# Two transposes of k and q on VectorE, each set some instructions later in the queue

## The chip, the cores and the metric

The kernel runs on one core of a Trainium2 chip. The metric is the device time of one execution in microseconds (us), measured in repeated runs. TensorE is PE in the profile, VectorE is DVE, ScalarE is ACT, GpSimd is POOL and SyncE is SP. A DMA is issued by the queue of SP, ACT or POOL.

## The reference

An mLSTM cell over 4 batches of 8 heads, 768 positions and head size 40, and then a feed-forward network (FFN) on its output, 3072 rows of 320 numbers:

```python
for t in range(S):
    m_new = np.maximum(f_gate[:, :, t] + m, i_gate[:, :, t])
    f_stab = np.exp(f_gate[:, :, t] + m - m_new)
    i_stab = np.exp(i_gate[:, :, t] - m_new)
    C = f_stab * C + i_stab * outer(vt, kt)
    n = f_stab * n + i_stab * kt
    y[:, :, t] = sigmoid(o_gate[t]) * (C @ qt) / np.maximum(np.abs(n @ qt), 1.0)
...
h = np.maximum(x @ w_in, 0.0)          # (3072, 320) @ (320, 2048)
return (h * h @ w_out).astype(np.float32)
```

## The kernel before

The recurrence is computed in chunks of 128 positions. There are 24 chunks, six to a batch, numbered from 0 by `s`; the ninth chunk is chunk 8. Within a chunk the sum over positions is a masked product, as in attention. `scores(s)` multiplies k by q on PE into two PSUM banks (L587, L595). `weigh(s)` makes the decay weights W on ACT and POOL in the tile `A_bc` (L510, L479). `weighted(s)` multiplies scores by W on VectorE in two instructions (L609), and the result, P, stands in `A_bc`. `attend_begin(s)` and `attend_end(s)` multiply P by v and the carried state C by the scaled q, and form the new state, on PE (L801, L823, L835). Between these two lies a tiny VectorE instruction on one element (L792), which reads what `attend_begin` wrote last. PE's `attend_end` waits for it. The change's title calls it the marker.

The FFN works on groups of two chunks, `g`. `ffn1_open`, `ffn1_rows` and `ffn1_close` are the first product, done with seven block products instead of eight (L1140, L1173); `ffn2_fast` is the second, in four steps of two products each (L1061). VectorE adds and subtracts the partial results: L1077 for the second product, L1156, L1158 and L1192 to L1195 for the first, and L1056 for the sums of blocks.

From chunk 7 on, k and q come into the layout that the scores need in three steps. `pair_up(s)` copies them into the DRAM scratch `kq_rows`. `load_squares(s)` brings them back as 32x32 squares into the tile `kqT_b[s % 2]` with four DMAs (L399), from SP up to chunk 10, then from ACT for odd chunks and SP for even ones. `turn_kq(s)` turns the squares in place on VectorE:

```python
def turn_kq(s):
    t = kqT_b[s % NKT][:].rearrange("p n j t -> p (n j t)")
    nc.vector.transpose(t, t)
```

It is one instruction over 128 x 1024 numbers (L406) and waits for all four DMAs. `scores(s)` waits for it.

The order is written by hand. Each engine takes its instructions in the order of the program, and waits for the other engines by semaphores. The main loop runs over quarter steps `n`, with `s = 6 + n // 4` and `at = n % 4`. In the steps of an even chunk PE does one group's second product, in those of an odd chunk another group's first one (`fast`). From chunk `EARLY = 10` on the even chunks are `joined`: their scores and their `attend_begin` stand inside the FFN1 of the chunk before. Chunks 8 and 9 are where the loop passes from one order to the other:

- `n = 8` (`s = 8`, `at = 0`): scores of chunk 8, turn of chunk 9, P of chunk 8, then step 0 of the second product of group 1.
- `n = 9`: `attend_begin(8)`, scores of chunk 9, `attend_end(8)`; behind these, in SP's queue, the load of the numerators (`load_num(8)`, L878) and `load_squares(10)`.
- `n = 11`: turn of chunk 10, then step 3 of the second product of group 1, whose last sum is an L1077.
- `n = 12` (`s = 9`, `at = 0`): `ffn1_open(3, 0)`, with L1156 and L1158.
- `n = 13`: `attend_begin(9)` with its marker, `ffn1_rows`, scores of chunk 10, `attend_end(9)`.

Of the kernel before, what the change touches and what calls it, by code (L numbers as in the profile page):

```python
# [29 lines left out]
def kernel(  # L30
# [317 lines left out]
    def load(s):  # L348
        b, c = divmod(s, NB)
        (dk, sk), nat_q, vv = load_parts(s)  # L350
        if s < ROT:
            for dst, src in ((dk, sk), nat_q, vv) if s < KQ_SQ else ((dk, sk), vv):
                nc.sync.dma_start(dst, src[b, :, c * P : (c + 1) * P, :].rearrange("h p d -> p h d"))
            return
        load_k(s)
        load_v(s)
# [47 lines left out]
# [3 lines that stand above are left out]
# [159 lines left out]
    def scores(s, o=(False, False)):  # L566
        d = st[s]

        sc = [bank(o[i]) for i in range(2)]
        d["sc"] = sc  # L570
        if s >= KQ_SQ:
            if s >= ROT:
                d["sc"] = [t.rearrange("p j t -> p (j t)")[:, : 3 * P].rearrange("p (e t) -> p e t", e=2) for t in sc]
            for e in range(2):
                for late_keys in range(2):
                    for c in range(2):
                        for i in range(2):
                            rows = slice(DP * i, DP * i + D)
                            start = e == late_keys == 0
                            if s < ROT:  # L580
                                j, keys = 2 * late_keys + e, HALVES[c]
                                to, t0 = sc[i][HALVES[c], j, :], 0
                            else:
                                j, keys = 2 * (c ^ late_keys) + e, HALVES[late_keys]
                                to = d["sc"][i][HALVES[c], e, slice(0, DP) if late_keys else slice(DP, 3 * DP)]
                                t0 = DP * late_keys
                            nc.tensor.matmul(  # L587
                                to, lhsT=d["kT"][rows, j, keys], rhs=d["qT"][rows, j, t0:], start=start, stop=True,
                                skip_group_check=True,
                            )  # L590
            return
        for j in range(PR):
            for i in range(2):
                rows = slice(DP * i, DP * i + D)
                nc.tensor.matmul(  # L595
                    sc[i][:, j, :], lhsT=d["kT"][rows, j, :], rhs=d["qT"][rows, j, :], start=True, stop=True,
                )
# [285 lines left out]
    def normalise_turned(s):  # L883
        d = st[s]
        N = d["N"].rearrange("p (e half m i r) -> p e half m i r", e=2, half=2, m=2, r=SQ)
        R = D - SQ
        den = N[:, :, 1, :, :, R]
        dm = work.tile([P, H], F32, name="dm")
        dm2 = dm[:].rearrange("p (m e i) -> p e m i", m=2, e=2)
        nc.vector.tensor_scalar(dm2, den, scalar1=-1.0, scalar2=1.0, op0=ALU.mult, op1=ALU.max)  # L890
        nc.vector.tensor_tensor(dm2, dm2, den, op=ALU.max)
        nc.vector.reciprocal(dm[:], dm[:])
        x = d["x"] = work.tile([P, 3 * P], F32, name="x_sb")
        x3 = x[:, :DM].rearrange("p (h d) -> p h d", d=D)
        x4, og = [
            t.rearrange("p (m e i) d -> p e m i d", m=2, e=2) for t in (x3, d["og"])
        ]
        for e in range(2):
            nc.vector.tensor_tensor(x4[:, e, :, :, :SQ], N[:, e, 0], og[:, e, :, :, :SQ], op=ALU.mult)
        for e in range(2):  # L900
            nc.vector.tensor_tensor(x4[:, e, :, :, SQ:], N[:, e, 1, :, :, :R], og[:, e, :, :, SQ:], op=ALU.mult)
        nc.vector.tensor_tensor(x3, x3, dm[:].unsqueeze(2).to_broadcast([P, H, D]), op=ALU.mult)
        nc.vector.tensor_copy(x[:, DM:], x[:, DM - KR : DM])
# [25 lines left out]
    def store_rows(s):  # L929
        t = st[s]["xT"] = xT_half(s).rearrange("p c t -> p (c t)")  # L930
        nc.sync.dma_start(x_d[s].rearrange("c t d -> t c d"), st[s]["x"][:].rearrange("p (c d) -> p c d", c=3))

    def load_rows(s):
        t = st[s]["xT"]
        for r in range(P // SQ):
            nc.sync.dma_start(
                t[r * SQ : (r + 1) * SQ].rearrange("p (b a) -> p b a", a=SQ),
                x_d[s, :, :, r * SQ : (r + 1) * SQ].rearrange("c (n p) a -> p (c n) a", p=SQ),
            )

    def turn_squares(s):
        t = st[s]["xT"]
        nc.vector.transpose(t, t)  # L943
        del st[s]
# [86 lines left out]
    def sums_of_weights(i):  # L1031
        if i < 3:
            T[i] = late.tile([P, NPAIR, DH], F32, name=f"T{i}", bufs=1)[:]
        if i == 0:
            nc.vector.tensor_tensor(T[0], B12, B11, op=ALU.subtract)
        elif i == 1:
            nc.vector.tensor_tensor(T[1], B22, T[0], op=ALU.subtract)
        elif i == 2:
            nc.vector.tensor_tensor(T[2], B21, T[1], op=ALU.subtract)
        else:  # L1040

            nc.vector.tensor_tensor(B12, B22, B12, op=ALU.subtract)
# [118 lines left out]
    def ffn1_rows(g, q, first):  # L1161
        xT, xs = st["xT", g], st["xs"]
        X, Y, V, Z = st["f1"]
        lo, hi = HALVES
        pairs = (
            ((X, lo, xT[lo, 0, 2, :], False), (Y, hi, xT[hi, 1, 2, :], first)),
            ((V, lo, xT[lo, 1, 2, :], first), (Z, hi, xs[hi, 1, :], False)),
        )
        for pair in pairs:
            for n in range(4):  # L1170
                for cols in HALVES:
                    for to, rows, rhs, start in pair:
                        nc.tensor.matmul(  # L1173
                            to[cols, n, :], lhsT=w_in2[rows, 4 * q + n, cols], rhs=rhs,
                            start=(start and n == 0), stop=True, skip_group_check=True,
                        )
# [36 lines left out]
    def do(f, s):  # L1213
        if 0 <= s < NT:
            f(s)
# [97 lines left out]
    for u in range(8):  # L1313
        s = 2 + u // 2
# [119 lines left out]
    EARLY = 10  # L1434
    assert ROUNDED[-1] == len(pieces)

    def joined(s):
        return EARLY <= s < NT and s % 2 == 0

    for n, (which, g, i) in enumerate(parts):  # L1440
        s, at = NB + n // 4, n % 4
# [11 lines left out]
                load_rows(s)  # L1453
        if at == 0 and even and s < EARLY:
            do(scores, s)
            if n > 0:
                do(turn_kq, s + 1)
            do(weighted, s)
        if n == 0:
            turn_kq(7)  # L1460
            pair_up(8)
# [3 lines left out]
        if at == (0 if joined(s) else 1):  # L1465
            if not joined(s):
                do(attend_begin, s)
            if n == 5:
                sums_of_weights(3)
            if even:  # L1470
                do(lambda s: scores(s, ("h" if s < EARLY else False, "h")), s + 1)
            if fast:
                ffn1_rows(g, 0, True)
                if joined(s + 1):
                    scores(s + 1, (False, "h"))
            do(attend_end, s)
            do(decays, s + 1)
            if not even and s > EARLY + 1:
                do(half_tanh, s)
            do(mask, s + 1)  # L1480
            if not even and not fast:
                do(turn_kq, s + 1)
            do(decay_C, s + 1)
            if not fast and not even:
                do(turn_squares, s - 1)
            if s == NB + 2:
                load(s + 3)
            do(store_num, s)
            if s > NB + 1:
                do(load_A, s + 2)  # L1490
            if n == 1:
                normalise_turned(5)
                store_rows(5)
                turn_squares(4)
            if n == 5:
                load_rows(6)
            do(load_num, s)
            if n == 1:
                load_rows(5)
                weigh(7, masked=True)  # L1500
                sums_of_win(2)
            if s + 2 <= EARLY:
                do(load_squares, s + 2)
            if even and s <= NB + 1:
                do(load_A, s + 2)
# [16 lines left out]
        if at == 2 and not fast:  # L1522
            if even and n > 2 and not joined(s):
                do(turn_squares, s - 1)
            do(scale_q, s + 1)
        if at == (1 if joined(s) else 3) and joined(s + 2):
            turn_kq(s + 2)
        if at == 3:
            if s % 4 == 3 and s < EARLY:
# [119 lines left out]
```

## Time and profile before

| | |
|---|---|
| median of 3 runs (lowest, highest) | 489.75 us (489.66, 490.23) |
| the profiled execution's own time | 489.91 us |
| its span, first to last instruction | 488.2 us |
| mean granted clock of PE | 0.992 |
| busy: PE, DVE, ACT, POOL | 476.6, 344.1, 244.0, 224.9 us |
| turns of k and q, L406 | 17 of 1.23 to 1.25 us |

The profile is of one execution. Of its own time of 489.91 us, 1.7 us lie outside the span. An engine's timeline lists its instructions in order of start: start, duration, engine, line, operation, output and inputs, count, and in square brackets how long the engine was idle ahead of it and what ended that. The view of waits adds these idle times up by who waited for whom. The chain of waits follows the end of the span back to what released each step.

### The profile page before, as it was taken

To read this page: it belongs to the slowest core of one execution; us is meant where nothing else is said; L and a number is where in the kernel's file an instruction comes from. 1 tells how busy PE (TensorE), PEld (TensorE's weight loads), DVE (VectorE), ACT (ScalarE), POOL (GpSimd) and SP (SyncE) were. 2 spreads that over 40 slices of the span, in tenths; PEclk is the share of its full clock that TensorE was granted. 3 is DMA by queue.
4 is the path that set the end of the run, shared out by engine and by line. 5 is a ranking of instruction groups with operands and counts; after the bars stand their busy time and mean duration, and the time that the engine had idled before them with its cause. 6 is when DMAs were issued, how large, how long until landed. Compare 5 with 4: busy or idle time off the path is not lost.

```text
span 488.2 us, 15700 instructions
## 1 busy us (share of the span) xinstructions
PE 476.6 (98%) x6389; PEld 444.6 (91%) x6389; DVE 344.1 (70%) x725; ACT 244.0 (50%) x534; POOL 224.9 (46%) x337
## 2 busy tenths in 40 slices
PE   9989999999898999999999999999999999999997
PEld 5877788779798999999999999999999999999997
DVE  7959768888886974775876975965965957635441
ACT  4697897644641651652752751653653651514300
POOL 5454545567881876826746836734833111020000
PEclk9988999999999999999999999999999999999999
DMA  8999998779997698677677686696773322200000
GB/s 174 209 253 265 259 202 209 201 144 230 194 190 108 165 169 164 164 155 155 149 149 153 159 165 145 155 155 128 156 144 87 93 58 82 55 15 15 1 28 27
DMA packets 192839, 69.93 MB, mean 143 GB/s; under 512 B 158144, under 2 KB 181504, under 8 KB 192768
## 3 DMA queue, kind: packets, MB, share of 16 engines
q1 hardware_dynamic: 157424, 56.39, 51.7%
q0 software_dynamic: 6080, 10.16, 9.4%
q10 hardware_dynamic: 29264, 2.39, 4.7%
q8 instruction: 50, 0.82, 0.7%
q14 instruction: 21, 0.17, 0.1%
HBM read 55.69 MB, written 18.92 MB: 153 GB/s over the span
## 4 chain that ended last, share of the span: by engine, by line
PE 77%; DMA 10%; SPq 6%; DVE 3%; ACT 1%; issue 1%; POOL 0%; DVEq 0%; ACTq 0%; POOLq 0%
PE h_ps L1061 32%; PE h_ps L1140 22%; PE h_ps L1173 7%; PE h_ps L977 5%; DMA kqT<-kq_rows 3%; PE numT L823 3%; DMA kq<-in_q_dram 2%; PE numT L801 2%; SPq L399 2%; PE tp L587 1%; PE h_ps L988 1%; DMA xT<-x_rows 1%; PE numT L835 1%; DMA raw<-in_moe_w_in_dram 1%; SPq L206 1%
## 5 line engine op out<-in xcount | busy, mean ns | idle before, releaser
L1061 PE MATMUL h_ps<-T,S 128*128 128x160 f32 x352 | 51.6, 300 | 0.7 <-DVE S L1056 0.7
L1061 PEld LDWEIGHTS h_ps<-T,S 128*128 128x128 f32 x352 | 48.9, 190 | 1.1 <-PE h_ps L1061 0.9
L1061 PE MATMUL h_ps<-w_out,g 128*128 128x160 f32 x336 | 48.8, 302 | 0.0
L1061 PEld LDWEIGHTS h_ps<-w_out,g 128*128 128x128 f32 x336 | 46.2, 190 | 1.1 <-issue 0.5
L1077 DVE TENSOR_TENSOR y_sb<-y_sb,h_ps 128x160 f32<-128x160 f32 x44 | 14.0, 318 | 45.2 <-PE h_ps L1061 45.1
L1154 ACT COPY r_sb<-h_ps 128x512 f32<-128x512 f32 x20 | 11.7, 584 | 65.5 <-PE h_ps L1140 54.0
L1140 PE MATMUL h_ps<-xT,w_in 128*128 128x128 f32 x320 | 43.2, 278 | 0.0
L1140 PE MATMUL h_ps<-lent_t,w_in 128*128 128x128 f32 x320 | 42.3, 275 | 0.0
L1173 PE MATMUL h_ps<-xT,w_in 64*64 64x128 f32 x960 | 39.5, 272 | 1.8 <-DVE r_sb L1156 1.8
L1132 POOL TENSOR_TENSOR lent_t<-xT 128x128 f32<-128x128 f32 (+1 forms) x18 | 10.3, 592 | 66.7 <-DVE xT L943 50.6
L1140 PEld LDWEIGHTS h_ps<-xT,w_in 128*128 128x128 f32 x320 | 39.2, 192 | 1.6 <-issue 1.2
L375 POOL DMA_DIRECT2D va<-in_v_dram x64 | 39.3, 630 | 0.3 <-issue 0.3
L1140 PE MATMUL h_ps<-lent_t 128*128 128x128 f32 x320 | 39.1, 275 | 0.0
L1140 PEld LDWEIGHTS h_ps<-lent_t,w_in 128*128 128x128 f32 x320 | 39.0, 192 | 0.0
L1140 PEld LDWEIGHTS h_ps<-lent_t 128*128 128x128 f32 x320 | 37.3, 192 | 0.2 <-issue 0.2
L1173 PEld LDWEIGHTS h_ps<-xT,w_in 64*64 64x64 f32 x960 | 35.1, 133 | 2.6 <-DVE r_sb L1156 2.1
L510 ACT ACTIVATE A_bc<-A_bc,b_R 128x64 f32<-128x64 f32 (+1 forms) x128 | 35.6, 362 | 0.1
L1191 ACT ACTIVATE g<-h_ps 128x512 f32<-128x512 f32 x12 | 7.2, 597 | 53.6 <-PE h_ps L1140 36.3
L479 POOL TENSOR_SCALAR_AFFINE_SELECT A_bc<-A_bc 64x512 f32<-64x512 f32 x32 | 25.7, 802 | 17.0 <-ACT kq L497 15.8
L977 PE MATMUL h_ps<-xT,w_in 128*128 128x256 f32 x128 | 31.6, 402 | 0.0
L858 DVE STREAM_TRANSPOSE tn<-numT 128x256 f32<-128x256 f32 x36 | 14.0, 425 | 23.4 <-PE numT L801 15.5
L531 POOL TENSOR_TENSOR vw<-va,A_bc 128x328 f32<-128x328 f32 x13 | 11.5, 886 | 39.6 <-ACT A_bc L510 39.6
(231 smaller groups left out, 1213.5 us busy)
## 6 DMA issues: line engine op xcount, KB each, us to landing
A_bc<-a_slots SPq DMA_DIRECT2D x32, 256.0 KB, 4.3
kq<-num_rows SPq DMA_DIRECT2D x80, 64.0 KB, 3.1
num_rows<-tn SPq DMA_DIRECT2D x18, 256.0 KB, 2.4
raw<-in_moe_w_out_dram SPq DMA_DIRECT2D x7, 640.0 KB, 4.8
og<-in_o_gate_dram SPq DMA_DIRECT2D x24, 160.0 KB, 5.1
x_rows<-x_sb SPq DMA_DIRECT2D x20, 192.0 KB, 2.6
xT<-x_rows SPq DMA_DIRECT2D x80, 48.0 KB, 2.6
out_dram<-y_sb SPq DMA_DIRECT2D x23, 160.0 KB, 2.5
```

Of the source, the lines that this page charges most:

```text
L375: eng.dma_start(dst[HALVES[n], PR * (1 - late_keys) : PR * (2 - late_keys)], src[HALVES[late_keys], PR * m : PR * (m + 1)],)
L479: nc.gpsimd.affine_select(part, part, compare_op=ALU.is_ge, fill=-1e30, base=0, pattern=[[0, PR], [0, 2], [1, DP]], channel_multiplier=-1,)
L510: nc.scalar.activation(A[0][:, x, to], A[0][:, x, to], AF.Exp, bias=b_R[:, b, c, own, x : x + 1],)
L531: nc.gpsimd.tensor_tensor(d["vw"][:].rearrange("p (own x) d -> p own x d", own=2), d["va"][:].rearrange("p (own x) d -> p own x d", own=2) ...
L823: nc.tensor.matmul(d["numT"][m][DP * e : DP * e + wide, i, t0:], lhsT=va_w[s % NKQ][keys, at * D1 : at * D1 + wide], rhs=rhs, start=(s % N ...
L858: nc.vector.transpose(to[:, 2 * m : 2 * m + 2], d["numT"][m].rearrange("p c t -> p (c t)"))
L977: nc.tensor.matmul(hs[i][:, n, :], lhsT=w_in[:, a, fb * P : (fb + 1) * P], rhs=xT[:, :, a, :], start=(n == 0 and a == 0), stop=False,)
L1061: nc.tensor.matmul(to, lhsT=lhsT[:, p], rhs=rhs[:, p, :], start=(start and p == 0), stop=(p == NPAIR - 1), skip_group_check=True,)
L1077: add = lambda to, a, b: nc.vector.tensor_tensor(to, a, b, op=ALU.add)
L1140: nc.tensor.matmul(to[:, n, :], lhsT=lhsT[:, 4 * q + n, :], rhs=rhs, start=(start and n == 0), stop=True, skip_group_check=True,)
L1154: nc.scalar.copy(m1[:], X[:])
L1173: nc.tensor.matmul(to[cols, n, :], lhsT=w_in2[rows, 4 * q + n, cols], rhs=rhs, start=(start and n == 0), stop=True, skip_group_check=True,)
```

## The change

Two calls of `turn_kq` move. At `n = 8` the P of chunk 8 now stands ahead of the turn of chunk 9. The turn of chunk 10 leaves its place at `n = 11`, ahead of the last step of the second product of group 1, and stands at `n = 13` right behind `attend_begin(9)`, so behind its marker and ahead of the scores of chunk 10. The turns of chunks 12 and on stay where they were. No instruction is added or taken away.

```diff
         if at == 0 and even and s < EARLY:
             do(scores, s)
+            do(weighted, s)
             if n > 0:
                 do(turn_kq, s + 1)
-            do(weighted, s)
...
         if at == (0 if joined(s) else 1):
             if not joined(s):
                 do(attend_begin, s)
+            if s + 1 == EARLY:
+                turn_kq(EARLY)
...
-        if at == (1 if joined(s) else 3) and joined(s + 2):
+        if at == 1 and joined(s) and joined(s + 2):
             turn_kq(s + 2)
```

## The prediction, made before the changed kernel had run

> **What bounds the kernel now.** I read the page first: PE is busy 98% of the span, so what there is to win is PE's idle time, 11.6 us. Next I read the view of waits for PE alone. Its two longest lines are
>
> ```profile
> PE h_ps L1173 <- DVE r_sb L1156: 1.8, 1, 1.8
> PE numT L801 <- DVE A_bc L609: 1.8, 1, 1.8
> PE h_ps L1061 <- DVE S L1056: 0.7, 1, 0.7
> PE numT L835 <- DVE kq L792: 0.7, 2, 0.5
> ```
>
> The first two occur once each, and PE waits for VectorE in both. VectorE's timeline at these two places, 131 and 152 us, tells what VectorE did instead:
>
> ```profile
> 130.39 0.68 DVE L1195 TENSOR_TENSOR g_c<-r_sb,h_ps 128x512 f32<-128x512 f32 x1
> 131.61 1.25 DVE L406 STREAM_TRANSPOSE kqT<-kqT 128x1024 f32<-128x1024 f32 x1 [0.54 <-DMA kqT<-kq_rows]
> 132.78 0.98 DVE L609 TENSOR_TENSOR A_bc<-tp,A_bc 128x384 f32<-128x384 f32 x2
> 133.68 1.20 DVE L1056 TENSOR_TENSOR g<-g 128x1024 f32<-128x1024 f32 x1
> 134.81 0.31 DVE L1077 TENSOR_TENSOR y_sb<-h_ps,y_sb 128x160 f32<-128x160 f32 x1
> 135.15 0.16 DVE L792 TENSOR_SCALAR kq<-numT 1x1 f32<-1x1 f32 x1
> ...
> 149.54 0.69 DVE L903 COPY x_sb<-x_sb 128x64 f32<-128x64 f32 x1
> 151.87 1.25 DVE L406 STREAM_TRANSPOSE kqT<-kqT 128x1024 f32<-128x1024 f32 x1 [1.63 <-DMA kqT<-kq_rows]
> 153.03 0.28 DVE L1077 TENSOR_TENSOR y_sb<-y_sb,h_ps 128x160 f32<-128x160 f32 x1
> 153.24 0.68 DVE L1156 TENSOR_TENSOR r_sb<-h_ps,r_sb 128x512 f32<-128x512 f32 x1
> ```
>
> Both times the queue stands on a turn (L406) that waits for its DMAs, and the instruction PE needs is queued behind it. PE's timeline shows the two stops from the other side:
>
> ```profile
> 131.17 0.43 PE L801 MATMUL numT<-kq,C 40*64 40x128 f32 x2
> 133.35 0.33 PE L801 MATMUL numT<-kq,C 40*64 40x128 f32 x3 [1.75 <-DVE A_bc L609]
> 134.27 0.88 PE L587 MATMUL h_ps<-kqT 40*64 40x128 f32 x32
> 135.36 0.44 PE L835 MATMUL numT<-vw,kq 64*64 64x41 f32 x16 [0.21 <-DVE kq L792]
> ...
> 151.73 0.41 PE L1173 MATMUL h_ps<-xT,w_in 64*64 64x128 f32 x2
> 153.97 1.11 PE L1173 MATMUL h_ps<-xT,w_in 64*64 64x128 f32 x31 [1.84 <-DVE r_sb L1156]
> ```
>
> The chain of waits for the second place names what sets the time: a load of `kqT` issued at 147.72 lands at 151.84, and the turn, L1077, L1156 and PE follow. From 157 us on PE has only 1.4 us of waits up to the end of the span, so a microsecond won here should reach the end.
>
> **Edit 1, P of chunk 8 ahead of the turn of chunk 9.** Nothing is added; on VectorE two L609 change places with one L406. PE stands still because one of `attend_begin(8)`'s banks holds scores that the first L609 still has to read. With the new order that L609 starts when L1195 ends, at 131.07, since scores (PE, done by 126.6) and W (ACT, done by 121.5) are there. PE goes on after 0.52 more, at 131.65 instead of 133.35. That would be 1.7 us, but it does not stay won. VectorE's list up to the marker is the same list: L609 twice (0.90 from start to start), L406 (1.17), L1056 (1.13), L1077 (0.34), from 131.07: the marker starts at 134.61, not 135.15. What is gone is only the 0.54 us of waiting, because the DMAs of chunk 9 (landed at 131.48) are there when the turn's place comes, at 131.97. PE would have the scores of chunk 9 to do at 132.6, waits for the turn's end at 133.2, is through at 134.1, and then waits for the marker: L835 at 134.82 instead of 135.36. So 1.75 us of stall turn into two shorter ones, and the gain is **0.54 us**. Were the DMAs late by more than 0.5 us, that excess would be taken off.
>
> **Edit 2, the turn of chunk 10 behind the marker.** At the old place the queue loses the wait and the turn, from 150.23 to 153.03. L1077 can start at 150.24 (its product ended before 147.3), L1156 at 150.45, ending 151.15; L1158 ends by 151.95. PE's `ffn1_rows` comes at 151.73 and needs no wait any more. In place of the gap from 151.79 to 153.97, 2.18 us, nothing is left. A second way gives the same: from the start of L801 to the restart of L1140 or L1061 chunk 9 took 150.82 to 157.21, 6.39 us, and chunk 11, with the same instructions and no stall, 166.33 to 170.46, 4.13. The difference of 2.26 holds 0.1 of other spacing; I take **2.19**.
>
> At the new place the turn stands behind L792, which fires when PE has ended `attend_begin(9)`, at 151.95 (151.53 and 0.39, and the usual few hundredths). So the turn starts at 152.17 (0.19 behind L792, as between 168.30 and 168.49) and ends at 153.42. Queued behind it are only the L858 of `attend_end(9)`, which wait for PE until 155 anyway. Who waits for it is PE's scores of chunk 10, due 1.77 us after 151.73 (the length of `ffn1_rows` in chunk 11), at 153.50. Cover and turn are equal within 0.1 us, so this turn is hidden, but barely: each tenth that it comes later is a tenth on PE.
>
> What can make it later is its DMAs. They landed at 151.84, 0.33 us ahead of 152.17. But edit 1 draws PE 0.54 earlier, and the turn then comes due at 151.63. The loads move along only in part: the third of them was issued when a load from ACT for chunk 11 had landed (issued 142.25, 5.04 us under way), and that one waits for VectorE's L763, which follows PE. At best they land at 151.30, at worst still at 151.84, which is 0.21 late. I take half of it, **0.1 us lost**.
>
> A rule bears on that term. The Trainium skill, "DMA: Bandwidth & Descriptors", section "Anatomy of one DMA", gives about 2.0 us and the bytes over 436 GB/s for a transfer. By it the last load, of 32 KB, would take an estimated 2.1 us where the trace has 4.12, the turn would never be late, and the sum would be larger by the 0.1. The measurement decides.
>
> One cost the trace does not show: L1077, L1156 and L1158 now run beside POOL's L479 (149.52 to 150.98). The bounds are none and, by the L1056 at 143.25 that took 3.48 us beside POOL instead of 1.22, 1.3 us more for L1156. The nearest row is the L1195 at 197.01, which also reads PSUM and one SBUF tile and took 0.68 beside POOL's L531 at 197.18, as all twenty L1195 did; so I take none. The other end makes the turn about 1.3 us later and leaves 0.9 of the 2.19.
>
> The Trainium skill, "SBUF — State Buffer", section "Who interferes with whom", speaks of a lock that blocks one of the two for a whole instruction. It exempts a VectorE instruction with at most one SBUF input outside the two-port modes, which these three are; read without the exemption it would speak against this edit, with the 1.3 us just named.
>
> On PE, ACT, POOL and SP the order stays. In the built program some transfers around chunk 13 use each other's completion semaphores; each still waits for one issued well ahead of it, at no cost that I can see.
>
> **Sum.** 489.91 - 0.54 - 2.19 + 0.1 = 487.28 for the profiled execution; the median lies 0.16 below that execution, so 487.1.
>
> **The rivals.** *The gain is trimmed*: the turn of chunk 10 is later than assumed, by the DMAs or by POOL, up to 1.3 us, and PE waits at its scores. 487.4 to 488.5. For it: the cover is only 0.1 us. Against: the rows above. *Both stalls vanish whole*: 1.7 and 2.19, 485.9. It would need a marker that does not bind; VectorE's list forbids it. *Given back later*: PE's next stops are at 206.06 (0.49 us, for a marker) and 209.79 (0.70, for L1056), behind VectorE's L890, which waits 2.24 us for numerators that land at 203.85. If those landed at the same clock time however early PE is, the stop would grow by what was won: 489.75. Against: their store is issued behind L858, which follows PE. *Slower*: the turn of chunk 10 now stands straight ahead of PE's scores, with no work behind it to fill the time. PE is back at the time of before when the scores start at 155.69, that is when the last load lands at 154.4, 2.5 us later than it did. It took 4.12 us of at most 7.3 for any of these loads. At 7.3 from the old issue it lands at 155.0, 0.6 slower, 490.4; if ACT's load ahead of it also took 7.3, 2.9 slower, 492.6. Nothing in the change makes DMAs slower, so this is unlikely. That the change does not do what it says is excluded: the built VectorE queue has exactly these moves.
>
> **How the numbers follow.** A change under 0.2%, 1.0 us, cannot be told from none. The forecast has 0.70, trimmed 0.14, both stalls whole 0.03, given back 0.07, slower 0.06. Faster by over 0.2% are the first three less the end of the trimmed case, 0.86; same 0.08; slower 0.06. The forecast's own spread is 486.7 to 487.4, from the bounds of the DMA term and the few tenths of spacing; with the trimmed case the range is 486.6 to 488.5.
>
> **What would show it.** In the changed kernel's PE timeline L801 should stop for 0.3 to 0.5 us near 131, scores of chunk 9 start near 133.2 and L835 at 134.8; L1173 should have no wait on L1156; scores of chunk 10 should start near 153.0 and L1140 near 154.6. VectorE's turn of chunk 10 should start between 151.6 and 151.9, without or with a short DMA wait. The span should be near 485.6. I am wrong if PE's wait at the scores of chunk 10 is over 0.5 us, if the marker near 134.6 does not move, or if PE's waits from 157 us on grow beyond 1.4.

## The result, and the profile after

The changed kernel took 486.82 us (median of 22 runs, 483.17 to 490.96), the kernel before 489.32 beside it (22 runs, 486.14 to 493.51). The ratio is 0.9958 (95% interval 0.9940 to 0.9975), a gain of 2.06 us with 1.2 to 2.9 as its interval. The medians lie 2.50 apart; the ratio is the better figure, since it leaves out a few disturbed runs. Forecast was a gain of 2.6 us. The profiled execution took 486.8 us, with a span of 485.1.

PE's waits in the changed kernel, each with its total, its count and its longest, in us:

```profile
PE numT L835 <- issue: 1.4, 1, 1.4
...
PE h_ps L1061 <- DVE S L1056: 0.9, 1, 0.9
...
PE numT L835 <- DVE kq L792: 0.5, 1, 0.5
PE h_ps L587 <- DVE kqT L406: 0.5, 1, 0.5
```

The waits of L1173 for L1156 and of L801 for L609, 1.8 us each before, are gone. Two waits of 0.5 have come; the 1.4 at the top is a new stop elsewhere, of which more below. VectorE's timeline (start, duration, and in brackets the idle time ahead of it):

```profile
128.83 0.68 DVE L1195 TENSOR_TENSOR g_c<-r_sb,h_ps 128x512 f32<-128x512 f32 x1
129.43 1.01 DVE L609 TENSOR_TENSOR A_bc<-tp,A_bc 128x384 f32<-128x384 f32 x2
130.36 1.23 DVE L406 STREAM_TRANSPOSE kqT<-kqT 128x1024 f32<-128x1024 f32 x1
131.52 1.18 DVE L1056 TENSOR_TENSOR g<-g 128x1024 f32<-128x1024 f32 x1
132.62 0.31 DVE L1077 TENSOR_TENSOR y_sb<-h_ps,y_sb 128x160 f32<-128x160 f32 x1
132.96 0.16 DVE L792 TENSOR_SCALAR kq<-numT 1x1 f32<-1x1 f32 x1
...
147.58 0.68 DVE L1156 TENSOR_TENSOR r_sb<-h_ps,r_sb 128x512 f32<-128x512 f32 x1
148.37 0.69 DVE L1158 TENSOR_TENSOR r_sb<-h_ps,r_sb 128x512 f32<-128x512 f32 x1
149.79 0.16 DVE L792 TENSOR_SCALAR kq<-numT 1x1 f32<-1x1 f32 x1 [0.73 <-PE numT L835]
149.98 1.25 DVE L406 STREAM_TRANSPOSE kqT<-kqT 128x1024 f32<-128x1024 f32 x1
```

The list up to the marker (L792) stands there without a gap, as forecast, and the turn of chunk 10 starts straight behind its marker and waits for nothing. PE beside it:

```profile
131.64 1.00 PE L587 MATMUL h_ps<-kqT 40*64 40x128 f32 x32 [0.50 <-DVE kqT L406]
133.17 0.44 PE L835 MATMUL numT<-vw,kq 64*64 64x41 f32 x16 [0.53 <-DVE kq L792]
...
148.63 0.45 PE L801 MATMUL numT<-kq,C 40*64 40x128 f32 x8
...
149.54 1.17 PE L1173 MATMUL h_ps<-xT,w_in 64*64 64x128 f32 x33
151.33 0.29 PE L587 MATMUL tp<-kqT 40*64 40x128 f32 x1
```

Clock times of two executions cannot be subtracted here. The two profiles of before reach the L1195 ahead of chunk 8's P at 130.39 and 128.38 us, the two of the changed kernel at 128.83 and 126.36: up to there one kernel differs from itself by 2.0 and 2.5 us, as much as the change brings. So I measure lengths inside an execution. *Stretch 1* goes from the start of that L1195 to the start of `attend_end(8)`'s L835, *stretch 2* from the start of chunk 9's first L801 to PE's restart at L1140, and the *rest* from that L1195 to the start of the last row of L1061. All runs in us, from their timelines:

| Kernel | stretch 1 | stretch 2 | PE's longest wait in stretch 2 | rest |
|---|---|---|---|---|
| before | 4.97 | 6.39 | 1.84 | 352.56 |
| before again (b1) | 5.33 | 6.24 | 1.69 | 352.65 |
| changed | 4.34 | 4.31 | 0 | 351.04 |
| changed again (a1) | 4.35 | 5.38 | 0.82 | 350.95 |
| e1, edit 1 alone | 4.35 | 7.11 | 2.55 | 353.33 |
| e2, edit 2 alone | 4.63 | 5.34 | 0.85 | 352.53 |
| e3 | 3.54 | 5.68 | 1.20 | 350.66 |
| e4 | 4.53 | 10.82 | 3.99 | 359.99 |
| e5 | 4.34 | 11.36 | 4.51 | 356.08 |
| e6 | 3.89 | 12.65 | 5.53 | 360.73 |
| e7 | 4.35 | 8.54 | 3.08 | 353.51 |
| e8 | 4.34 | 4.31 | 0 | 350.07 |
| e9 | 3.53 | 4.88 | 0.34 | 351.38 |

### The profile page after: what moved, and what is told of

The parts are those of the page before. It is cut to its first block, busy times and chain, and to the rows that moved or that the text cites. A ratio compares the mean times of both kernels' runs of the same rounds, so it can differ in the third digit from the quotient of the medians.

```text
span 485.1 us, 15702 instructions
## 1 busy us (share of the span) xinstructions
PE 473.7 (98%) x6387; PEld 442.2 (91%) x6389; DVE 343.4 (71%) x725; ACT 243.4 (50%) x534; POOL 225.3 (46%) x337
## 4 chain that ended last, share of the span: by engine, by line
PE 57%; DVE 0%; issue 0%
PE h_ps L1061 28%; PE h_ps L1140 18%; PE h_ps L1173 5%; PE numT L823 2%; PE numT L801 1%; PE tp L587 1%; PE numT L835 1%; DVE S L1056 0%; PE h_ps L587 0%; DVE g L1195 0%; DVE y_sb L1077 0%
## 5 line engine op out<-in xcount | busy, mean ns | idle before, releaser
L1061 PE MATMUL h_ps<-T,S 128*128 128x160 f32 x352 | 51.6, 299 | 0.9 <-DVE S L1056 0.9
L1061 PEld LDWEIGHTS h_ps<-T,S 128*128 128x128 f32 x352 | 48.9, 190 | 1.1 <-PE h_ps L1061 1.1
L1061 PE MATMUL h_ps<-w_out,g 128*128 128x160 f32 x336 | 48.8, 301 | 0.0
L1061 PEld LDWEIGHTS h_ps<-w_out,g 128*128 128x128 f32 x336 | 46.2, 190 | 1.1 <-issue 0.5
L1140 PE MATMUL h_ps<-xT,w_in 128*128 128x128 f32 x320 | 43.3, 278 | 0.0
L1140 PE MATMUL h_ps<-lent_t,w_in 128*128 128x128 f32 x320 | 42.3, 275 | 0.0
L1140 PEld LDWEIGHTS h_ps<-xT,w_in 128*128 128x128 f32 x320 | 39.2, 192 | 1.6 <-issue 1.2
L1173 PE MATMUL h_ps<-xT,w_in 64*64 64x128 f32 x960 | 39.3, 272 | 0.0
L1140 PE MATMUL h_ps<-lent_t 128*128 128x128 f32 x320 | 39.1, 275 | 0.0
L1140 PEld LDWEIGHTS h_ps<-lent_t,w_in 128*128 128x128 f32 x320 | 38.9, 192 | 0.0
L1140 PEld LDWEIGHTS h_ps<-lent_t 128*128 128x128 f32 x320 | 37.3, 192 | 0.2 <-issue 0.2
L1173 PEld LDWEIGHTS h_ps<-xT,w_in 64*64 64x64 f32 x960 | 35.1, 133 | 0.6
L479 POOL TENSOR_SCALAR_AFFINE_SELECT A_bc<-A_bc 64x512 f32<-64x512 f32 x32 | 25.6, 800 | 16.0 <-ACT kq L497 14.8
L977 PE MATMUL h_ps<-xT,w_in 128*128 128x256 f32 x128 | 29.9, 386 | 0.4 <-POOL w_in L236 0.4
```

Of the source, the lines that this page charges most:

```text
L479: nc.gpsimd.affine_select(part, part, compare_op=ALU.is_ge, fill=-1e30, base=0, pattern=[[0, PR], [0, 2], [1, DP]], channel_multiplier=-1,)
L977: nc.tensor.matmul(hs[i][:, n, :], lhsT=w_in[:, a, fb * P : (fb + 1) * P], rhs=xT[:, :, a, :], start=(n == 0 and a == 0), stop=False,)
L1061: nc.tensor.matmul(to, lhsT=lhsT[:, p], rhs=rhs[:, p, :], start=(start and p == 0), stop=(p == NPAIR - 1), skip_group_check=True,)
L1140: nc.tensor.matmul(to[:, n, :], lhsT=lhsT[:, 4 * q + n, :], rhs=rhs, start=(start and n == 0), stop=True, skip_group_check=True,)
L1173: nc.tensor.matmul(to[cols, n, :], lhsT=w_in2[rows, 4 * q + n, cols], rhs=rhs, start=(start and n == 0), stop=True, skip_group_check=True,)
```

## The experiments

Each ratio below is to the kernel before, run beside that version. The stretches are those of the one profiled execution of each version; in e1, e4, e5 and e6 it was slower than the median of the runs, in e4 and e6 the slowest of all. Some expectations count stretch 1 from the end of L1195, which makes it 0.68 us less.

**Each edit alone.** e1 is the kernel before with edit 1:

```diff
@@ at == 0 and even and s < EARLY
             do(scores, s)
+            do(weighted, s)
             if n > 0:
                 do(turn_kq, s + 1)
-            do(weighted, s)
```

> Edit 1 alone: P of chunk 8 ahead of the turn of chunk 9; the turn of chunk 10 at its old place. Theory (the marker binds, so only VectorE's 0.54 us of waiting for DMAs is won): from the end of L1195 to the second L835 of chunk 8 3.7 us, as with both edits, instead of 4.3; from the start of L801 of chunk 9 to the restart of L1140 still 6.4 us; time 0.4 to 0.7 us below the kernel before. Rival (PE's whole stall at L801 is won): the first stretch 2.6 us and the time 1.7 us below.

Measured: 490.39 us (12 runs), ratio 0.9999 (0.9961 to 1.0037). Stretch 1 came out as expected, 4.35. Stretch 2 grew to 7.11. VectorE in e1:

```profile
152.25 1.25 DVE L406 STREAM_TRANSPOSE kqT<-kqT 128x1024 f32<-128x1024 f32 x1 [3.35 <-DMA kqT<-kq_rows]
```

The turn of chunk 10 at its old place waited 3.35 us for its loads, where it had been 1.63 before. Some 1 us of the difference is not edit 1's: the L1056 at 142.91 took 1.77 us, where it took 3.48 before, so VectorE came to the turn sooner. PE's own wait grew by 0.71 us, from 1.84 to 2.55. In this execution what edit 1 had won went into a longer wait for a DMA that did not come earlier. The 0.4 to 0.7 us expected in the time lie within the interval, and so does no gain at all.

e2 is the kernel before with edit 2:

```diff
+            if s + 1 == EARLY:
+                turn_kq(EARLY)
...
-        if at == (1 if joined(s) else 3) and joined(s + 2):
+        if at == 1 and joined(s) and joined(s + 2):
```

> Edit 2 alone: the turn of chunk 10 behind the marker; turn of chunk 9 ahead of P of chunk 8, as before. Theory (the turn and its DMA wait held up L1156, and at the new place PE's first-product rows cover it): from L801 of chunk 9 to the restart of L1140 4.3 us, as with both edits; first stretch, end of L1195 to L835, still 4.3 us where the DMAs of chunk 9 land late; time 2.0 to 2.2 us below the kernel before. Rival (the gain needs both edits, since edit 1 gives the loads their room): the second stretch over 5 us.

Measured: 488.0 us (12 runs), ratio 0.9996 (0.9964 to 1.0027). Stretch 1 was 4.63, with only 0.20 of wait at the turn of chunk 9; stretch 2 was 5.34, a gain of 1.05 over the first profile of before instead of 2.1. The time missed the expectation too: at most 1.8 us of gain lie in the interval, and 2.0 to 2.2 were expected. VectorE in e2:

```profile
149.24 0.16 DVE L792 TENSOR_SCALAR kq<-numT 1x1 f32<-1x1 f32 x1 [0.77 <-PE numT L835]
150.44 1.25 DVE L406 STREAM_TRANSPOSE kqT<-kqT 128x1024 f32<-128x1024 f32 x1 [1.04 <-DMA kqT<-kq_rows]
```

The turn stands where it should, but its loads land 1.04 us after the marker, and PE waits 0.85 at the scores of chunk 10. That is the mechanism of the prediction's rival "trimmed". The sign of e2's own rival, a second stretch over 5 us, is there as well, but its reason does not hold: a1, next, has edit 1 and the same late loads.

**The changed kernel and the kernel before once more.**

> The changed kernel unaltered, profiled once more. My theory (stretch 1 is set by VectorE's list, stretch 2 by when the last load of chunk 10 lands): stretch 1 is 4.3 us again, within 0.1; stretch 2 is 4.3 plus what the landing is later than the marker, 0 to 1.2 us. Rival (the lengths of both stretches are the code's alone, and e2 and e3 differ because of their own edits): stretch 2 is 4.3 again, whatever the landing.

a1 took 485.47 us (12 runs), ratio 0.9962 (0.9933 to 0.9991). Stretch 1 was 4.35, stretch 2 was 5.38. VectorE in a1:

```profile
147.33 0.16 DVE L792 TENSOR_SCALAR kq<-numT 1x1 f32<-1x1 f32 x1 [1.06 <-PE numT L835]
148.50 1.25 DVE L406 STREAM_TRANSPOSE kqT<-kqT 128x1024 f32<-128x1024 f32 x1 [1.02 <-DMA kqT<-kq_rows]
```

So the same code shows the late landing of e2 in one execution and none in another: the rival, lengths fixed by the code, falls. SP's issues of chunk 10's loads in a1 (their number, the shortest, median and longest in ns, the first and last start in us, and below it the time from issue to landing):

```profile
L399 SPq DMA_DIRECT2D kqT<-kq_rows x4: 303/394/922, 138.1 to 142.6; - x4
...
DMA to landing us min/median/max: 5.1/5.8/6.0
```

The last issue is 3.56 us ahead of chunk 9's L801 (146.16) here and 3.33 ahead in the first profile (145.3 and 148.63, shown with e8 below), so it was not later. What differs between the two is the time from issue to landing, 5.1 to 6.0 us against 4.1 to 4.9. What made it longer was not tried apart.

> The kernel before, unaltered, profiled once more. My theory (the stop at L1173 follows the landing of chunk 10's loads, which shifts by 1 to 2 us from one execution to the next): stretch 1 is 4.4 us plus what the turn of chunk 9 waits for its DMA, and stretch 2 is 4.3 us plus 0.9 to 1.6 and what the turn of chunk 10 waits for its DMA, 6 to 7.2 in all. Rival (the two lengths are fixed): 4.97 and 6.39 again, within 0.1.

b1 took 487.97 us (one run). Stretch 1 was 5.33 with a DMA wait of 0.89, so the rival of fixed lengths falls. Stretch 2, 6.24, lies in the 6 to 7.2 expected, but not by the sum given there: the turn of chunk 10 waited 2.07 us (put down in the trace to a store, `x_rows<-x_sb`), which would make over 7. Take the DMA wait off stretch 1 in the three profiles that list one ahead of chunk 9's turn: 4.97 - 0.54, 5.33 - 0.89 and e2's 4.63 - 0.20 all give 4.43 or 4.44. The list of VectorE is fixed and the DMA comes on top, which is what edit 1 takes away.

**What binds stretch 1.** e3 is the changed kernel with one L1056 (`sums(1, ..., (3,))`) taken from ahead of the marker of chunk 8 to behind it:

```diff
             if n == 9:
+                sums(1, slice(0, NPAIR), (3,))
...
-        if n == 8:
-            sums(1, slice(0, NPAIR), (3,))
```

> Both edits, and the 1.2 us sum L1056 (g<-g) of group 1, which stands ahead of the marker of chunk 8, set behind it. Theory (VectorE's list up to the marker is what is left of the first stall): the marker comes 1.1 us earlier, PE's L835 of chunk 8 then follows the scores of chunk 9 without a wait, and the stretch from the end of L1195 to L835 falls from 3.7 to 3.1 us; time 0.6 us below the changed kernel. Rival (PE is held there by the turn of chunk 9 or by something else than the marker): the stretch stays at 3.7. What could take it back: L1056 now stands ahead of L858, whose late end would delay the next steps; theory says it is hidden, since L858 waited 1.0 us for PE.

Measured: 488.6 us (12 runs), ratio 0.9981 (0.9945 to 1.0017). Stretch 1 shrank by 0.80 to 3.54, and PE's wait for the marker was gone: VectorE's list ahead of the marker did bind. Stretch 2 was 5.68, because the turn of chunk 10 waited 1.15 us for its loads, and because the marker of chunk 9 came 1.41 us behind its L801, where it was 1.16 in the changed kernel. The rest, 350.66, is 0.3 to 0.4 below that of the changed kernel, too little to show in the times.

**How much cover the new place has.** e7 does the turn of chunk 10 three times over:

```diff
             if s + 1 == EARLY:
-                turn_kq(EARLY)
+                for _ in range(3):
+                    turn_kq(EARLY)
```

> The changed kernel with the turn of chunk 10 done three times over, on the same data, at its new place behind the marker. It measures how much cover that place has. My theory (cover and turn are equal within 0.1 us, so every further turn stands on PE's path): PE waits about 2 x 1.17 = 2.3 us at the scores of chunk 10 (0.85 to 1.2 us more if the loads land late as in e2 and e3), the stretch from L801 to L1140 grows from 4.3 to 6.6 us, and the time by 2.3 us. Rival (there is slack behind the turn, so that it was hidden with room to spare): PE's wait grows by under 1 us and the stretch stays under 5.3.

Measured: 488.38 us (10 runs), ratio 1.0031 (1.0000 to 1.0062). Its VectorE timeline, and then its PE timeline:

```profile
148.46 3.80 DVE L406 STREAM_TRANSPOSE kqT<-kqT 128x1024 f32<-128x1024 f32 x3 [0.72 <-DMA kqT<-kq_rows]
```

```profile
152.36 0.29 PE L587 MATMUL tp<-kqT 40*64 40x128 f32 x1 [3.08 <-issue]
```

PE's idle time is put down to "issue", but the turns' end at 152.26 (148.46 and 3.80) is what it follows. The turns were 0.72 us late and 2.55 (3.80 less 1.25) longer; PE waited 3.08 of those 3.27, so the cover is 0.19 us, against 0.1 in the prediction. a1 (1.02 late, 0.82 waited) and e2 (1.04, 0.85) give 0.20 and 0.19, and so does e3 with its late marker (1.15 and 0.25 late, 1.20 waited: 0.20). The rival of room to spare falls. Stretch 2 grew by more than the wait, to 8.54; the last section tells why.

**Loading chunk 10 earlier.** e4 is the kernel before with the squares of chunk 10 issued ahead of chunk 8's numerators:

```diff
+            if s + 2 == EARLY:
+                do(load_squares, s + 2)
             do(load_num, s)
...
-            if s + 2 <= EARLY:
+            if s + 2 < EARLY:
```

> The kernel before with one change: SP issues the loads of chunk 10's squares ahead of the numerators of chunk 8 (L878) instead of behind them; both turns at their old places. Theory (of the 2.18 us of stall at L1173, 1.63 are the turn's wait for DMAs and the rest is the turn itself): the turn of chunk 10 has no DMA wait, PE's stall at L1173 falls to about 0.5 us, from L801 of chunk 9 to the restart of L1140 4.8 us; time 1.5 to 1.7 us below the kernel before. Rival (the DMAs of this stretch share the engines, so an earlier issue lands no earlier, or the numerators become the late ones): the stretch stays above 6 us, or L890 gets a DMA wait of over 1 us.

Measured: 491.83 us (7 runs), ratio 1.0087 (1.0052 to 1.0122). The turn of chunk 10 had no wait any more, but VectorE in e4 met another ahead of it, as the rival said:

```profile
149.32 0.17 DVE L890 TENSOR_SCALAR dm<-kq 128x8 f32<-128x8 f32 x1 [4.40 <-DMA kq<-num_rows]
```

The numerators became the late ones, and PE waited 3.99 us. e5 does the same to the changed kernel, with the loads also ahead of the numerators' store:

```diff
+        if n == 8:
+            load_squares(EARLY)
...
-            if s + 2 <= EARLY:
+            if s + 2 < EARLY:
```

> The changed kernel, with the four loads of chunk 10's k and q on SP issued ahead of chunk 8's numerators (store and four loads) instead of behind them. My theory (the change as a whole; what is left to chance is when chunk 10's k and q land): the turn of chunk 10 never waits for a DMA, and the stretch from the start of chunk 9's L801 to the restart at L1140 is 4.3 us in every execution. If the numerators of chunk 8 are still in time, the median is 0 to 0.8 us below the changed kernel's. Rival (the two sets of loads contend for SP's queue and for completions shared with ACT's loads, so that the one put second is the one that is late): L890 waits for the numerators, by some 4 us as in e4, and the stop that it makes on PE costs 2 to 4 us: 489 to 491.

Measured: 490.67 us (12 runs), ratio 1.0072 (1.0042 to 1.0102). L890 waited 7.39 us, PE 4.51: the rival held. e6 puts e3 and e5 together.

> The kernel of e3 (both edits, and L1056 of chunk 8's sums behind the marker) with the early loads of e5 on top. My theory (the marker of chunk 8 binds stretch 1, chunk 10's loads bind stretch 2, and the two are independent): stretch 1 is 3.6 us as in e3, stretch 2 is 4.3 instead of e3's 5.68, and the median is some 0.7 us below the changed kernel's. Rival (the numerators become the late ones): stretch 1 is 3.6 all the same, but L890 waits for its numerators, and the time is 2 to 4 us above the changed kernel's.

Measured: 491.92 us (12 runs), ratio 1.0099 (1.0067 to 1.0130), with the same stop (7.40 at L890, 5.53 on PE). Stretch 1, at 3.89, stayed short, though not the 3.6 expected.

**Why chunk 10 lands late.** e8 leaves the order of SP's queue and moves ACT's loads for chunk 11 to SP, behind chunk 10's:

```diff
-                do(lambda s: load_squares(s, nc.scalar), s + 3)
+                do(lambda s: load_squares(s, nc.sync if s == EARLY + 1 else nc.scalar), s + 3)
```

> The changed kernel with the four loads of chunk 11's k and q issued by SP, behind chunk 10's, instead of by ACT. So far SP's third load of chunk 10 is issued only when ACT's first load for chunk 11 has landed, because the two use one completion semaphore; here they no longer do. My theory (that shared semaphore sets the landing of chunk 10, and so PE's wait at its scores): SP issues chunk 10's four loads within some 1.5 us of each other instead of 4.5 to 6, they land ahead of the marker, VectorE's turn of chunk 10 waits for no DMA, and stretch 2 is 4.3 us. The median would be 0 to 0.8 us below the changed kernel's. Rival (the transfers themselves are slow, since the 16 DMA engines are busy most of the time here, and issuing them earlier only makes them take longer): the landing stays 1.3 to 2.7 us behind the start of chunk 9's L801, the turn waits up to 1 us as in the other runs, and stretch 2 is 4.3 to 5.7.

SP's issues of chunk 10's loads, read as in a1, in the changed kernel:

```profile
L399 SPq DMA_DIRECT2D kqT<-kq_rows x4: 302/339/566, 139.8 to 145.3; - x4
...
DMA to landing us min/median/max: 4.1/4.4/4.9
```

and in e8:

```profile
L399 SPq DMA_DIRECT2D kqT<-kq_rows x4: 365/708/1727, 139.8 to 142.7; - x4
...
DMA to landing us min/median/max: 4.0/4.4/4.8
```

Both begin at 139.8. Without the completion semaphore shared with ACT's load the last issue comes 2.6 us earlier, though the four still lie 2.9 us apart and not the 1.5 expected. The transfers take no longer than in this profile of the changed kernel, which speaks against the rival. It does not show that the issue alone sets the landing: a1's longer transfers made it late as well. The loads land by some 147.5 (142.7 and 4.8), ahead of the marker at 149.88. Stretch 2 is 4.31. In the changed kernel the last was issued at 145.3 and took at least 4.1, so it landed at 149.4 or later, at most 0.6 us ahead of the turn at 149.98. The time was 487.3 us (12 runs), ratio 0.9978 (0.9947 to 1.0008); its rest is the shortest of all, 350.07, but the runs do not tell e8 from the changed kernel.

e9 puts e3 and e8 together.

> The kernel of e3 (both edits, L1056 of chunk 8's sums behind the marker) with chunk 11's loads on SP as in e8. My theory: both stretches are short at once, stretch 1 3.6 us and stretch 2 4.3, so 5 to 6 of the 11.4 us of before's two stretches... in sum 7.9 us against 11.36 before and 8.65 in the changed kernel's first profile; the median is 0.7 us or somewhat more below the changed kernel's. Rival (the sum at its later place, or SP's longer list of loads, makes something else late): a new wait of over 0.5 us on PE between 133 and 165 us, and a time no lower than the changed kernel's.

Measured: 489.14 us (12 runs), ratio 1.0010 (0.9982 to 1.0038). The two stretches, 3.53 and 4.88, were shorter in sum than the changed kernel's 8.65, though stretch 2 was not the 4.3 expected: VectorE came to the marker late, and PE waited 0.34. The rival's new wait came a chunk later. VectorE's timeline, and then PE's, in e9:

```profile
167.57 0.17 DVE L890 TENSOR_SCALAR dm<-kq 128x8 f32<-128x8 f32 x1 [3.53 <-DMA kq<-num_rows]
```

```profile
169.75 0.44 PE L835 MATMUL numT<-vw,kq 64*64 64x41 f32 x16 [2.16 <-DVE kq L792]
```

Chunk 10's numerators were late in this execution; what held them was not tried apart. No version was shown to beat the changed kernel.

## Why the prediction was right, point by point

*The bound.* That PE's two stops could be won held. That what is won reaches the end held in a1: the stretches are 0.62 and 1.01 us shorter than in before's first profile, and 1.61 of these 1.63 are there at the last L1061. It did not hold in e2, whose stretches are 1.39 shorter in sum and whose rest is only 0.03 shorter. PE's stops behind stretch 2 are 0.68 us longer in e2 (0.89, 0.70 and 0.48, against 0.49, 0.70 and 0.20 before); the other 0.68 are in no stop that the view lists, and their cause is open.

*Edit 1.* Forecast 0.54, the DMA wait alone; measured 0.63 (4.97 to 4.34). Most of the 0.09 is in one row: L609 starts 0.60 us behind the start of L1195 (128.83 and 129.43), where the prediction had the whole 0.68 of L1195. (Its 0.52 from there to PE's restart should be 0.58, for 131.65; the sum does not use it.) The claim that 1.75 us of stall turn into shorter ones because the marker binds is shown by e3. Where I expected a short wait at L801, none is listed: its instructions are only drawn out, and PE loses 0.50 before the scores of chunk 9 and 0.53 before L835. The size is that of one execution: stretch 1 is 4.43 us and the DMA wait of chunk 9's turn without the edit, 4.35 with it, so it is worth 0.28 at e2's wait of 0.20 and 0.97 at b1's 0.89. And alone nothing of it is seen at the end of e1's profile, where the next DMA takes it.

*Edit 2.* 2.19 less 0.1 were forecast, 2.08 measured in the first profile, and 1.01 in a1. The place is right as well: the turn starts 1.35 us behind the start of chunk 9's L801, as worked out (151.63 less 150.28). The price of POOL was taken as none, and L1156 and L1158 took 0.68 and 0.69 beside POOL's L479 (147.33 to 148.79). Here the trace agrees with the Trainium skill, "SBUF — State Buffer", section "Who interferes with whom", and its exemption for such instructions.

*The step that was mis-sized* is the term of the DMAs: "At best they land at 151.30, at worst still at 151.84 ... I take half of it, 0.1 us lost". Its bounds came from one execution's landing. PE's wait at the scores of chunk 10 was 0 in the first profile, 0.82 in a1, and 0.85 and 1.20 in e2 and e3, where the turn stands at the same place. So the condition that I had set for being wrong, over 0.5 us there, is met by the second profile of the changed kernel, and "trimmed", at 0.14, was too unlikely: it is what some executions do. Two things set the landing, and the prediction had each from one execution only: when SP issues the last load, behind one of ACT's (e8), and how long the load then takes, which is what differs between the two profiles of the changed kernel. A gain of 2.06 us where 2.63 were summed fits such a loss in part of the executions, though its interval reaches 2.9. The rule of the Trainium skill, "DMA: Bandwidth & Descriptors", section "Anatomy of one DMA", which made an estimated 2.1 us and no late turn, is given there for DMAs issued by GpSimd; these are issued by SP, and took 4.0 to 6.0 us to landing in the changed kernel, a1 and e8.

*The rest of the first profile.* 2.71 us are won in the two stretches and 1.52 at the last L1061. The difference is mainly one stop of 1.41 us on PE at 227.19, in the middle of a group of sixteen L835, with no releaser in the trace ("issue"). e4 has one of 1.40 at 235.03, in the middle of such a group too, and the other eleven profiles have none of this kind. What causes it stays open. It is not the rival "given back", which named 206 and 209: those stops, 0.49 and 0.70 before, were 0 and 0.34 in b1, 0 and 0.85 in the first profile and 0.85 and 0.70 in a1, so they change from one execution to the next. But another sign of being wrong that I had set, waits of PE from 157 us on beyond 1.4, is met by both profiles of the changed kernel: 2.26 and 1.55 us.

*What was luck.* The span, forecast near 485.6, was 485.1, but 1.56 us of the 3.1 that it is shorter lie ahead of the L1195 (130.39 and 128.83), where the change does nothing. And 486.82 lies so near 487.1 because the kernel before took 489.32 this time and not the 489.75 that the sum started from, while the gain by the ratio is 0.6 smaller than forecast.

*The slower rival* needed loads 2.5 us later than before and did not come. Its price was too low, though: e7 had a wait of 3.08, and its stretch 2 grew by 4.23.

## What to carry to other kernels

When an in-order engine stands on a DMA, count the list behind it up to the next instruction that PE needs: only the wait is won, not the stall that it shows as. Moving work off a DMA's landing makes the landing the next limit, so take its spread from several executions, and look at what holds back the issue (here a semaphore shared with another queue's load) before issuing earlier: a load put ahead in a shared queue made another one late three times out of three. Where a kernel's start-up varies by more than the change brings, compare lengths inside an execution.

## What the runs showed of the hardware that I had not expected

A wait of PE can cost more than its length. Granted clock (the column of 1.00, 0.51, 0.50) in e7, around the wait of 3.08 us; the columns are the window, its length, busy time and number of instructions of PE, PEld, DVE, ACT and POOL, the clock, the DMA share and GB/s:

```profile
152.30:152.80 0.50, 0.44 (x14) 0.47 (x18) 0.00 (x0) 0.00 (x0) 0.00 (x0) 1.00 0.99 303
152.80:153.30 0.50, 0.50 (x23) 0.50 (x18) 0.00 (x0) 0.00 (x0) 0.00 (x0) 0.51 0.19 64
...
155.80:156.30 0.50, 0.50 (x4) 0.50 (x4) 0.32 (x3) 0.00 (x0) 0.03 (x1) 0.57 0.00 0
156.30:156.80 0.50, 0.50 (x7) 0.50 (x6) 0.00 (x0) 0.06 (x1) 0.43 (x1) 1.00 0.14 53
```

Half a microsecond after PE's restart the clock fell to 0.50 and stayed there for some 3.4 us. After the waits of 3.99, 4.51 and 5.53 us (e4, e5, e6) it was at 0.50 from the restart on, and the first 32 L1173 took 1.98 or 1.99 us; after the waits of 1.84 (before) and 2.55 us (e1) the clock stayed at 1.00, and 31 of them took 1.11 and 1.12.

The length of the wait alone does not decide, though. Later in e4, at the marker of another chunk, a much shorter stop was enough:

```profile
208.78 0.44 PE L835 MATMUL numT<-vw,kq 64*64 64x41 f32 x16 [1.65 <-DVE kq L792]
```

The clock is at 0.50 from 209.2 to 212.6 there, and the sixteen L1061 behind it take 3.95 us, where such a row takes 2.3 to 2.4 at a clock of 1.00. e6 has the same behind a stop of 1.75 at 209.34 (4.11 us), while e9's 2.16 left the clock at 1.00. What decides was not tried apart.

What the low clock costs inside stretch 2 is read from its length, less 4.31 us and less the wait. 1.15 us are left in e7 (8.54 - 4.31 - 3.08), 2.5 in e4 and e5 and 2.8 in e6; where the clock stayed at 1.00, 0.17 to 0.25 are left as well (before, b1, a1, e1, e2, e3). So the clock's part is 0.9 to 1.0 us in e7, 2.3 in e4 and e5 and 2.6 in e6. The Trainium skill, "TensorE: Matmul & The Clock Gate", section "What's actually happening", tells of half the rate after an idle window of about 3.4 us; here it followed stops of 3.08 and even of 1.65 us. The slower rival's price left this cost out.
